# Attention with its products with v issued in one burst per chunk of queries

## The chip, the cores and the metric

The kernel runs on one core of a Trainium2 chip. The metric is the device time of one launch in microseconds (us). TensorE is called PE below, VectorE DVE, ScalarE ACT, GpSimd POOL, and SyncE, which issues the DMAs here, SP.

## What is computed

Three parts follow each other: attention with rotary embedding over 2 batches, 8 heads, 576 tokens and head size 64; a gated layer on 1152 tokens; and a layer of eight experts whose weights come from eight rounds of row and column scaling. The change is in the attention alone:

```python
scores = scale * np.matmul(q_rot, k_rot.transpose(0, 1, 3, 2))
scores = scores - np.max(scores, axis=-1, keepdims=True)
attn = np.exp(scores)
attn = attn / (np.sum(attn, axis=-1, keepdims=True) + 1e-09)
return np.matmul(attn, v).astype(np.float32)
```

## The kernel before

Attention goes through 8 pairs of heads (n = 0 to 7). A pair's 2 x 576 queries are nine units u of 128 rows: u = 0 to 3 are the two heads' first 256 queries (chunk c = 0), u = 4 holds the last 64 queries of both heads, and u = 4 to 8 make chunk c = 1.

The work of a unit u, with the short names used from here on:

- **s(u)**, L272, PE: the scores into one of two PSUM tiles of the pool ps_s (2 banks each).
- **max(u)**, L277, DVE: the negated row maximum, read from that tile.
- **exp(u)**, L293, ACT: the exponential, read from that tile, which is free afterwards.
- **t(u)**, L312, PE: four transposes of the probabilities into one of two PSUM tiles of ps_t.
- **copy(u)**, L327: that tile to SBUF, on ACT for u = 0, 2, 6 and on DVE for the others.

For each chunk there are also: **rest** (L334 to L338, PE transposes of leftover keys) with its copy **q** (L343, DVE); **spread** (L369, L371, PE) with its copy **rc** (L375, ACT), which lays out the inverse sums; the products with v, **pv** (L384, PE), five groups j = 0 to 4 of two matmuls (one per head, into the lower and the upper 64 partitions); **xf** (L393, DVE), which scales them; and, once a pair, **xh** (L399, ACT) and **xl** (L67, POOL). The operands of later pairs are made beside it: multiplications and an addition on POOL (L214, L218), the **hl cast** (L224, ACT), the **hl subtraction** (L67, DVE or POOL) and SP's DMAs that stack them (L246 to L252). The conversion of the next part's first weights (L134 to L150) also runs during pairs 2 to 4.

The order is a table: `at(step, slot, ...)`. Pair n starts at step 9n, and in each step the slots are emitted in order. On PE a step holds s(u), then t of two units earlier, then rest, then spread, then pv:

```python
SLOTS = ["load", "pe0", "dve0", "act0", "act1", "dve1", "dve2", "pe1", "pe2", "pe3", ...]
t0 = b + 5 + 5 * c
for j in range(5):
    at(t0 + VALUES[c][j], "pe3", values, n, c, j)
at(t0 + SUMMED[c], "dve3", summed, n, c)
```

So chunk 0 has its products from the step of u = 7 on, and they end in the step of the next pair's u = 0; chunk 1 has them from the next pair's u = 3 to its u = 5. PE, POOL and SP keep the written order. On DVE and ACT the scheduler moves some instructions, as the rows below show.

Of the kernel before, what the change touches and what calls it, by code (L numbers as in the profile page):

```python
# [42 lines left out]
LOAD_V = -2  # L43
REST = (1, 0)
SPREAD = (1, 2)
VALUES = ((2, 2, 4, 4, 4), (2, 2, 4, 4, 4))
SUMMED = (5, 5)
ACT_TURNS = (0, 2, 6)
CONVERSIONS = (18, 32)
# [8 lines left out]
def fused(ctx, tc, qk, v, rope, wgv, wo, wg2, w1, w2, out):  # L58
# [109 lines left out]
    def attention(xT, W):  # L168
        with ExitStack() as st:
# [236 lines left out]
            def at(step, slot, fn, *args):  # L406
                plan.setdefault((max(step, FIRST), SLOTS.index(slot)), []).append((fn, args))
# [5 lines left out]
            for n in range(pairs):  # L413
# [26 lines left out]
                for c in range(2):  # L440
# [8 lines left out]
                    for j in range(5):  # L449
                        at(t0 + VALUES[c][j], "pe3", values, n, c, j)  # L450
                    last = n == pairs - 1
# [457 lines left out]
```

## Time and profile before

| | |
|---|---|
| time, median of 3 runs | 1163.0 us (1162.06 to 1171.15) |
| profiled execution: time, span | 1172.19 us, 1170.4 us |
| PE busy | 1146.6 us, 98% of the span |
| DVE, ACT, POOL busy | 816.7, 392.3, 89.9 us |
| attention | first 174 us of the span |
| granted TensorE clock, mean of the span | 0.983 |

The page's chain of work that ended last is PE for 91% of the span. In PE's timeline each row gives start, duration, engine, line, output and inputs, shapes, and the count; a matmul of the program stands there as two records, so four transposes read x4 while four matmuls of pv read x8. A duration includes the time in which a result drains out of the array, so the distance between starts, not the duration, is what an instruction costs PE.

### The profile page before, as it was taken

How to read it: one execution, taken by the hardware profiler on the slowest of the kernel's cores; microseconds unless marked ns; L12 is line 12 of the kernel's file. 1: busy time of each engine (PE TensorE's matmuls, PEld its weight loads, DVE VectorE, ACT ScalarE, POOL GpSimd, SP SyncE). 2: the span in 40 equal slices, each digit the busy share in tenths (PEclk: the TensorE clock that was granted, in tenths of full speed). 3: DMA queues.
4: the chain of work that ended last, by engine and by line, in shares of the span. 5: the costliest groups of instructions: out<-in, count | busy, mean ns of one | idle time of the engine just before them, and what ended most of it. 6: DMA issues, size and time to landing. Idle time of an engine off the chain costs nothing.

```text
span 1170.4 us, 17008 instructions
## 1 busy us (share of the span) xinstructions
PE 1146.6 (98%) x6840; PEld 1033.4 (88%) x6840; DVE 816.7 (70%) x1420; ACT 392.3 (34%) x656; POOL 89.9 (8%) x88
## 2 busy tenths in 40 slices
PE   7999999999999998999999999999999999999998
PEld 6776768999999987998989989989899899898997
DVE  6588767997875477866857758568577585685763
ACT  4476654443432344321312213213122132131220
POOL 5467500000000000000000000000000000000000
PEclk7799999999999999999999999999999999999999
DMA  4767604332222011111111111111111111111002
GB/s 159 191 175 203 148 12 145 108 108 73 79 84 73 18 55 45 49 52 36 55 54 37 37 45 52 49 36 55 54 37 37 48 50 48 36 55 54 19 1 81
DMA packets 24991, 80.64 MB, mean 69 GB/s; under 512 B 4368, under 2 KB 4880, under 8 KB 23504
## 3 DMA queue, kind: packets, MB, share of 16 engines
q1 hardware_dynamic: 24912, 79.56, 22.7%
q8 instruction: 53, 0.87, 0.3%
q14 instruction: 26, 0.21, 0.1%
HBM read 64.80 MB, written 2.36 MB: 57 GB/s over the span
## 4 chain that ended last, share of the span: by engine, by line
PE 91%; DVE 4%; DMA 2%; issue 1%; ACT 1%; SPq 1%; POOL 0%; DVEq 0%; ACTq 0%
PE p L727 11%; PE p L725 11%; PE p L726 11%; PE s L272 4%; PE pv L384 3%; PE t L312 2%; PE po L163 2%; PE po L164 2%; PE po L165 2%; PE pg L165 2%; PE pg L163 2%; PE pv L165 2%; PE pg L164 2%; PE pv L164 2%; PE pv L163 2%
## 5 line engine op out<-in xcount | busy, mean ns | idle before, releaser
L725 PE MATMUL p<-wh,hh 128*128 128x512 f32 x576 | 224.9, 390 | 0.4 <-ACT hh L669 0.4
L727 PE MATMUL p<-wh,hl 128*128 128x512 f32 x576 | 224.5, 390 | 0.1
L726 PE MATMUL p<-wl,hh 128*128 128x512 f32 x576 | 224.4, 390 | 0.0
L100 ACT CAST wh<-raw 128x768 fp32r<-128x768 f32 (+1 forms) x96 | 94.1, 981 | 332.5 <-PE p L727 230.4
L737 DVE SCALAR_TENSOR_TENSOR acc<-p,Pm,acc 128x512 f32<-128x512 f32 x126 | 94.4, 749 | 146.6 <-PE p L727 146.6
L67 DVE TENSOR_TENSOR wl<-raw,wh 128x768 fp32r<-128x768 f32 (+1 forms) x96 | 108.4, 1130 | 36.4 <-ACT wh L100 34.9
L727 PEld LDWEIGHTS p<-wh,hl 128*128 128x128 f32 x576 | 108.1, 188 | 23.3 <-DVE hl L670 0.8
L725 PEld LDWEIGHTS p<-wh,hh 128*128 128x128 f32 x576 | 108.2, 188 | 22.6 <-ACT hh L669 0.9
L726 PEld LDWEIGHTS p<-wl,hh 128*128 128x128 f32 x576 | 108.2, 188 | 21.6
L669 ACT ACTIVATE hh<-d 128x1152 fp32r<-128x1152 f32 (+1 forms) x68 | 74.6, 1098 | 118.2 <-DVE d L674 118.2
L670 DVE SCALAR_TENSOR_TENSOR hl<-d,hh 128x1152 fp32r<-128x1152 f32 (+1 forms) x68 | 85.8, 1262 | 20.6 <-ACT hh L669 20.6
L277 DVE TENSOR_REDUCE ng<-s 128x1 f32<-128x576 f32 x72 | 54.0, 753 | 25.0 <-PE s L272 23.3
L293 ACT ACTIVATE p<-s,ng 128x576 f32<-128x576 f32 x64 | 47.6, 744 | 32.0 <-DVE ng L277 32.0
L111 DVE TENSOR_TENSOR raw<-raw 128x256 f32<-128x256 f32 x128 | 53.4, 417 | 0.6
L163 PE MATMUL pg<-xh,wh 128*128 128x384 f32 x144 | 48.9, 339 | 3.3 <-ACT wh L143 2.6
L165 PE MATMUL pg<-xh,wl 128*128 128x384 f32 x144 | 48.7, 338 | 0.0
L164 PE MATMUL pg<-xl,wh 128*128 128x384 f32 x144 | 48.6, 338 | 0.0
L164 PE MATMUL po<-ul,wh 128*128 128x384 f32 x144 | 48.4, 336 | 0.0
L165 PE MATMUL po<-uh,wl 128*128 128x384 f32 x144 | 48.4, 336 | 0.0
L163 PE MATMUL po<-uh,wh 128*128 128x384 f32 x144 | 48.4, 336 | 0.0
L164 PE MATMUL pv<-xl,wh 128*128 128x384 f32 x144 | 48.3, 335 | 0.0
L163 PE MATMUL pv<-xh,wh 128*128 128x384 f32 x144 | 48.3, 335 | 0.0
(3330 smaller groups left out, 2720.6 us busy)
## 6 DMA issues: line engine op xcount, KB each, us to landing
raw<-in_w SPq DMA_DIRECT2D x64, 512.0 KB, 3.9
raw<-in_wgv SPq DMA_DIRECT2D x11, 1024.0 KB, 4.8
x<-in_qk SPq DMA_DIRECT2D x15, 576.0 KB, 4.6
raw<-in_wo SPq DMA_DIRECT2D x12, 512.0 KB, 3.8
x<-hl SPq DMA_DIRECT2D x42, 144.0 KB, 3.4
x<-hl SPq DMA_DIRECT2D x14, 288.0 KB, 4.1
v<-in_v SPq DMA_DIRECT2D x8, 320.0 KB, 4.7
out<-acc SPq DMA_DIRECT2D x9, 256.0 KB, 2.0
```

Of the source, the lines that this page charges most:

```text
L67: (eng or nc.vector).tensor_tensor(out=out_, in0=a, in1=hi.bitcast(F32), op=ALU.subtract)
L100: nc.scalar.copy(out=hi[:, 0:n], in_=raw[:, 0:n])
L163: nc.tensor.matmul(ps, wh[wsl], xh[xsl], start=first, stop=False)
L164: nc.tensor.matmul(ps, wh[wsl], xl[xsl], start=False, stop=False)
L165: nc.tensor.matmul(ps, wl[wsl], xh[xsl], start=False, stop=last)
L277: nc.vector.tensor_reduce(out=R[n, u], in_=SC[n, u][:, :, 0:288], axis=AX.XY, op=ALU.max, negate=True)
L669: nc.scalar.activation(out=hh[:, f, ts], in_=src, func=AF.Relu)
L670: nc.vector.scalar_tensor_tensor(out=hl[:, f, ts], in0=src, scalar=0.0, in1=hh[:, f, ts].bitcast(F32), op0=ALU.max, op1=ALU.subtract)
L725: nc.tensor.matmul(po, hh[:, f, tl], wh[:, ws], start=f == 0, stop=False)
L726: nc.tensor.matmul(po, hh[:, f, tl], wl[:, ws], start=False, stop=False)
L727: nc.tensor.matmul(po, hl[:, f, tl], wh[:, ws], start=False, stop=f == 3)
L737: nc.vector.scalar_tensor_tensor(out=acc[:, t], in0=po, scalar=Pm[:, t, e:e + 1], in1=acc[:, t], op0=ALU.mult, op1=ALU.add)
```

## The change

The table VALUES gives for each of a chunk's five groups of products the step in which it is issued, counted from t0. Groups 0 and 1 go from t0 + 2 to t0 + 4, where groups 2, 3 and 4 already were.

```diff
-VALUES = ((2, 2, 4, 4, 4), (2, 2, 4, 4, 4))
+VALUES = ((4, 4, 4, 4, 4), (4, 4, 4, 4, 4))
```

On PE this is chunk 1 of pair 0, with pair 1's scores around it (p_396 and q_397 are the turned probabilities, x the stacked operands, hl and bd those of unit 4):

```order
 L371 MATMUL t<-fold,both 128x64
-L384 MATMUL pv<-p_396,v 64x320 x4
 L272 MATMUL s<-hl_273,bd_120 128x288 x6
 L312 MATMUL t<-ident,p 128x128 x4
 L272 MATMUL s<-x_288,x_296 128x288 x4
 L312 MATMUL t<-ident,p 128x128 x4
-L384 MATMUL pv<-p_396,v 64x320 x4
+L384 MATMUL pv<-p_396,v 64x320 x8
 L384 MATMUL pv<-q_397,v 64x320 x2
```

Four of the ten matmuls move behind s(4), t(2), s(5) and t(3). In chunk 0 they move in the same way behind s(8), t(6), the next s(0) and t(7). The last pair's chunk 1 already had its ten matmuls in a row, so 15 of the 16 chunks change.

On DVE the scheduler places one instruction differently. In the stretch of chunk 1 of pair 4, with pair 5's units, these rows stand before the change:

```order
L277 TENSOR_REDUCE ng<-s 128x1
L327 COPY p_1459<-t 128x4x128
L343 COPY q_1460<-rest 128x320
L277 TENSOR_REDUCE ng<-s 128x1 x2
L327 COPY p_1588<-t 128x4x128
L67 TENSOR_TENSOR hl_1522<-x,hl_1522 128x576
L352 RECIPROCAL sum<-sum 128x4
```

and these with it:

```order
L277 TENSOR_REDUCE ng<-s 128x1
L327 COPY p_1459<-t 128x4x128
L343 COPY q_1460<-rest 128x320
L67 TENSOR_TENSOR hl_1517<-x,hl_1517 128x576
L277 TENSOR_REDUCE ng<-s 128x1 x2
L327 COPY p_1588<-t 128x4x128
L277 TENSOR_REDUCE ng<-s 128x1
```

The rows are max(1), copy(8) and q, then max(2) and max(3), copy(1). The hl subtraction, which stood behind copy(1), now stands ahead of max(2). It is ahead of max(2) in the stretches of pairs 0, 1, 3, 4 and 5, behind max(2) in that of pair 2, and there is none in that of pair 6.

On ACT the same stretch read, before,

```order
L358 COPY iv<-sum 128x256
L360 ACTIVATE both<-mask,sum 128x128
L293 ACTIVATE p,sum<-s,ng 128x576
L327 COPY p_1588<-t 128x4x128
L224 CAST hl_1522<-x 128x576
L293 ACTIVATE p,sum<-s,ng 128x576
```

and now reads

```order
L358 COPY iv<-sum 128x256
L360 ACTIVATE both<-mask,sum 128x128
L224 CAST hl_1517<-x 128x576
L293 ACTIVATE p,sum<-s,ng 128x576
L327 COPY p_1588<-t 128x4x128
L293 ACTIVATE p,sum<-s,ng 128x576
```

The rows with L293 are exp(1) and exp(2). The hl cast has moved from behind copy(0) to ahead of exp(1). The rows of POOL and SP are the same in both kernels.

## Rows read from the trace of the kernel before

**Rows 1.** Windows: stretch, PE, PEld, DVE, ACT, POOL busy us, PEclk, DMA share, GB/s
```profile
20.00:45.00 25.00, 24.97 (x100) 19.01 (x98) 13.34 (x21) 11.98 (x30) 10.48 (x9) 0.50 0.61 160
...
120.00:145.00 25.00, 24.96 (x185) 18.66 (x184) 18.86 (x33) 18.52 (x47) 12.32 (x13) 1.00 0.62 154
```
**Rows 2.** Timeline of PE, s(1) of pair 5 to s(0) of pair 6
```profile
118.58 0.80 PE L272 MATMUL s<-x,x 128*128 128x288 f32 x4
...
120.01 0.78 PE L272 MATMUL s<-x,x 128*128 128x288 f32 x4
...
121.09 0.80 PE L272 MATMUL s<-x,x 128*128 128x288 f32 x4
...
122.65 1.30 PE L384 MATMUL pv<-p,v 128*64 128x320 f32 x8
123.88 1.06 PE L272 MATMUL s<-hl,bd 128*128 128x288 f32 x6
...
125.12 0.77 PE L272 MATMUL s<-x,x 128*128 128x288 f32 x4
...
128.18 0.80 PE L272 MATMUL s<-x,x 128*128 128x288 f32 x4
...
129.61 0.77 PE L272 MATMUL s<-x,x 128*128 128x288 f32 x4
130.43 0.65 PE L312 MATMUL t<-ident,p 128*128 128x128 f32 x4
131.01 1.08 PE L384 MATMUL pv<-p,v 128*64 128x256 f32 x8
132.03 0.80 PE L272 MATMUL s<-x,x 128*128 128x288 f32 x4
...
133.02 0.79 PE L272 MATMUL s<-x,x 128*128 128x288 f32 x4
```
**Rows 3.** Timeline of DVE in the same pair: max(1) to copy(4)
```profile
119.42 0.76 DVE L277 TENSOR_REDUCE ng<-s 128x1 f32<-128x576 f32 x1 [0.29 <-PE s L272]
120.09 0.68 DVE L327 COPY p<-t 128x512 f32<-128x512 f32 x1
120.69 0.48 DVE L343 COPY q<-rest 128x320 f32<-128x320 f32 x1
121.09 1.60 DVE L277 TENSOR_REDUCE ng<-s 128x1 f32<-128x576 f32 x2
...
123.20 0.75 DVE L67 TENSOR_TENSOR hl<-x,hl 128x576 fp32r<-128x576 f32 x1
...
129.69 0.68 DVE L327 COPY p<-t 128x512 f32<-128x512 f32 x1
```
**Rows 4.** Timeline of ACT in the same pair: exp(1), copy(0), exp(6) to exp(7)
```profile
120.21 0.74 ACT L293 ACTIVATE p<-s,ng 128x576 f32<-128x576 f32 x1 [1.22 <-DVE ng L277]
...
121.26 0.59 ACT L327 COPY p<-t 128x512 f32<-128x512 f32 x1 [0.22 <-PE t L312]
...
129.81 0.74 ACT L293 ACTIVATE p<-s,ng 128x576 f32<-128x576 f32 x1 [2.06 <-DVE ng L277]
...
130.79 0.68 ACT L399 CAST xh<-xf 128x576 fp32r<-128x576 f32 x1
131.37 0.68 ACT L224 CAST hl<-x 128x576 fp32r<-128x576 f32 x1
131.94 0.75 ACT L293 ACTIVATE p<-s,ng 128x576 f32<-128x576 f32 x1
```
**Rows 5.** Timeline of PE, the last pair's chunk 1, groups 0 to 3
```profile
171.05 2.39 PE L384 MATMUL pv<-p,v 128*64 128x320 f32 x16
```
**Rows 6.** Timeline of PE, chunk 0 of pair 0, groups 0 and 1, then 2 and 3
```profile
36.12 1.98 PE L384 MATMUL pv<-p,v 128*64 128x256 f32 x8
...
43.19 1.98 PE L384 MATMUL pv<-p,v 128*64 128x256 f32 x8
```
**Rows 7.** Timeline of POOL: the addition that the moved hl cast reads
```profile
118.60 1.43 POOL L218 TENSOR_TENSOR x<-x 128x576 f32<-128x576 f32 x1
```

## Prediction, made before the change was run

> **What bounds the kernel now.** I read the windows by stage first. In the steady attention (120 to 145 us) PE is busy 24.96 of 25.00 us at full clock, DVE 18.86 and ACT 18.52 [rows 1]. So PE carries the time there, but DVE and ACT are close enough that a chain through them can hold PE up for a part of a step. "Busy" doesn't show this, because short waits hide between matmuls that drain; the distances between starts do. Therefore the timelines come next, of PE [rows 2], DVE [rows 3] and ACT [rows 4], over one pair.
>
> The reader is to see one chain in them. The scores have two PSUM tiles, so s(3) can't start before exp(1) has read the tile of s(1). s(1) starts at 118.58, max(1) at 119.42, exp(1) at 120.21, s(3) at 121.09 [rows 2 to 4]: 0.84 + 0.79 + 0.88 = 2.51 us from s(u) to s(u + 2), with nothing queued in between. PE's own work in a step with no product and no rest is 0.99 us (132.03 to 133.02), so two such steps are worth 1.98 us and the chain is longer. Before the change few steps stand like that: the steps from s(3) to s(4) and from s(7) to s(8) carry the first burst, 1.23 us (122.65 to 123.88) and 1.02 us (131.01 to 132.03) [rows 2]. While PE multiplies by v, DVE and ACT catch up. The change empties just these two steps.
>
> **The bursts themselves.** It removes no matmul. Two bursts become one, and one change between scores and products less is paid per chunk. The last pair's chunk 1 already shows the merged form: 16 records take 2.39 us [rows 5], where 8 take 1.30 [rows 2]. So two bursts cost 2.60, one 2.39, and the saving is 0.21 us per chunk, 15 x 0.21 = 3.2 us if nothing else moved. Put the other way, the later burst grows by 2.39 - 1.30 = 1.09 us in chunk 1. For chunk 0 no merged form is in the trace; in proportion it grows by 1.08 x 1.09 / 1.30 = 0.91 us, with 1.02 (no saving at all) as the upper bound.
>
> **Chunk 0, walked from s(6) = 0** (128.18). exp(6) starts at 1.63, xh at 2.61, the hl cast for a later pair at 3.19, exp(7) at 3.76 [rows 4]. This queue of ACT hangs on s(6) and has the same order in the changed kernel, so exp(7) stays where it is although max(7) is done earlier. The next pair's s(0) needs its tile: 3.76 + 0.88 = 4.64. PE alone would be there sooner: s(7) at 1.43; t(5) at 2.25 as now, since it takes the PSUM tile that copy(4) empties (129.69 to 130.37 [rows 3], t(5) at 130.43 [rows 2]); then, without the burst, s(8) at 132.03 - 128.18 - 1.02 = 2.83, and s(0) 0.99 later at 3.82. So PE waits 0.82 us ahead of s(0). Before, s(0) came at 4.84. The gain is 0.20, the burst behind it grows by 0.91, net **+0.71 us**.
>
> **Chunk 1, walked from s(1) = 0** (118.58). DVE runs max(1) at 0.84, copy(8) at 1.51, q at 2.11 and is free at 2.51 [rows 3]. There max(2) stood; now the hl subtraction does, and it takes about the 0.67 us that DVE spends on max(1) (119.42 to 120.09; the row's 0.75 includes its drain) [rows 3]. max(2) starts at 3.18, exp(2) at 3.18 + 0.79 = 3.97, and s(4) at the earliest at 3.97 + 0.88 = 4.85. PE alone: s(3) at 2.51 plus 2.79 - 1.23 = 1.56, that is 4.07. So PE waits 0.78 us ahead of s(4). s(5) follows 1.24 later at 6.09; exp(3), with max(3) right behind max(2) at 3.85, needs to start by 6.09 - 0.88 = 5.21 and can. Before, s(5) came at 6.54. Gain 0.45, burst grows by 1.09, net **+0.64 us**. Where no hl subtraction is in the way, max(2) stays at 2.51, s(4) comes at 2.51 + 0.79 + 0.88 = 4.18 and s(5) at 5.42: gain 1.12, net 0.
>
> Behind max(2) on DVE stand max(3) and copy(1), and t(2) waits for copy(1)'s PSUM tile; by 4.52 + 0.60 = 5.12 it is free, while s(4)'s six matmuls, 1.06 us long [rows 2], run until 5.91, so nothing further is held. The moved hl cast on ACT goes ahead of exp(1), where ACT is idle for 1.22 us [rows 4]; I cost it at nothing as long as POOL's addition is done by then (rival C).
>
> **The sum over the chunks.** Chunk 1: pairs 0, 1, 3, 4, 5 have the subtraction ahead of max(2), 5 x 0.64 = 3.2; pair 2 has it behind, between 0 and 0.64, taken as 0.2; pair 6 has none, 0; pair 7 is unchanged. Chunk 0: pairs 1, 4, 5 at 0.71 make 2.1; in pairs 2 and 3 the weight conversion on DVE already holds PE up, so the new wait lies partly inside an old one, between 0 and 0.71, taken as 0.3 each; in pair 6 no hl cast follows xh, so exp(7) starts at 3.19, s(0) at 4.07, net 4.07 - 4.84 + 0.91 = +0.1; pair 7 has no further s(0), 0; pair 0 runs at half clock [rows 1], where PE's own steps are twice as long and the chain hides, 0. Total 3.2 + 0.2 + 2.1 + 0.6 + 0.1 = **+6.2 us**. Bounds: -3.2 (every wait hidden) and +9 (no saving per burst, and pairs 2 and 3 paying in full).
>
> What follows attention waits for the last xf, whose own chunk is unchanged, so the shift goes through to the end. The profiled execution took 1172.19 us (span 1170.4), which would become 1178.4. It is 9.2 us above the median of the runs, 1163.0; against that the forecast is 1163.0 + 6.2, or **1169 us**.
>
> **The clock in pair 0.** From 20 to 45 us PE was busy 24.97 of 25 us and the granted clock was 0.50, the lower of its levels, 1.2 GHz [rows 1]. The change gathers pair 0's chunk 0 there: the 1.98 us at 36.12 [rows 6] go behind, and the joined burst starts about 1.98 us earlier than 43.19. Beside this stands a rule: the Trainium skill, in "TensorE: Matmul & The Clock Gate", section "Why this matters for your kernels", says that keeping TensorE busy continuously brings it to full clock. By that rule a longer unbroken burst could only help; the row disagrees in so far as full busyness at 20 to 45 us did not raise the clock. The sum of +6.2 leaves the clock as it is; the other outcome is rival D.
>
> **The rivals.**
>
> A, the forecast: the emptied steps are held up by the chain through the two score tiles. 1169 us, with its own range 1164 to 1173. Chance 0.62.
>
> B: the waits don't appear, because the scheduler's new places let DVE and ACT keep up. Then only the saving is left, 1163.0 - 3.2 = 1160 us. For it: PE is the busiest engine by far. Against it: 2.51 us for two steps is read from the trace, not assumed, and ACT's queue ahead of exp(7) is unchanged. Chance 0.13.
>
> C, the slower side: the hl cast, now ahead of exp(1) on ACT, waits for POOL's addition, and the hl subtraction, now ahead of max(2) on DVE, waits for the cast; max(2) to s(4) queue behind both. Before, the addition ended 1.45 us after s(1) (118.60 + 1.43 [rows 7]) and nothing urgent stood behind it. It starts from xh, and xh comes earlier against s(1) than before by the 0.7 us of chunk 0, so it should end near 0.7; the cast (0.68) then ends at 1.4, and DVE wants it at 2.51. So it decides only once the addition ends after 2.51 - 0.68 = 1.83. If it comes at 2.8, every one of the five chunks pays 1.0 us more: +5, which gives 1174 us, and later by as much again 1179. For it: POOL carries conversion work too. Chance 0.17.
>
> D: the clock rises at the start of the joined burst in pair 0. Its 16 records take twice 1.98 us at half clock [rows 6]; at full clock half of that, 2.0 us less: 1163.0 + 6.2 - 2.0 = 1167 us. Against it: the same matmuls at 36.12 did not raise it. Chance 0.08.
>
> **How the numbers follow.** The predicted time is A's, 1169. The low end, 1161, leaves out most of B (0.10); the high end, 1177, leaves out the upper half of C (0.08). So 1161 to 1177 holds about 8 in 10. A measurement can tell about 1% of this kernel, 11.6 us, from no change: faster means below 1151.4, slower above 1174.6. No case lies below 1151; I leave 0.02 for it. Above 1174.6 lies about half of C, 0.09, and a share for the runs themselves, which differed by 9.1 us (1162.06 to 1171.15) with the same kernel, so that A's 1169 could be measured above the line: 0.10. Slower 0.19, same 0.79.
>
> **What would show it.** In the changed kernel's timeline of PE, s(6) to the next s(0) should be 4.64 us and s(1) to s(5) 6.09, s(5) to s(6) should grow from 3.06 to 4.15, and a steady pair as a whole should get 0.71 + 0.64 = 1.35 us longer. In DVE's timeline the hl subtraction should start about 2.5 us after s(1) and max(2) 3.2 after it. If s(0) comes at 3.82 and s(4) at 4.07, B holds. If max(2) starts later than 3.2 after s(1) with DVE idle ahead of the hl subtraction, C holds. If PEclk is 1.00 before 45 us, D. The forecast is wrong altogether if the scores' waits stay where they are and a steady pair gets shorter.

## The result, and the profile after

The median of 11 runs is 1171.86 us (1167.38 to 1178.65), against 1164.03 us (1162.06 to 1172.22) of 11 runs of the kernel before beside them. The ratio is 1.0058, with a 95% interval of 1.0036 to 1.0081. The change costs 7.8 us, a little over half a per cent, where +6.2 us was forecast; the median lies inside the forecast's range of 1161 to 1177.

The profiled execution took 1170.55 us, with a span of 1168.8 us and a mean granted clock of 0.991. Its page gives first the busy time of each engine, then the share of each engine in the chain of work that ended last:

```profile
PE 1138.7 (97%) x6840; PEld 1031.5 (88%) x6840; DVE 812.9 (70%) x1420; ACT 392.5 (34%) x656; POOL 89.8 (8%) x88
...
PE 87%; DVE 5%; ACT 3%; DMA 2%; issue 1%; SPq 1%; POOL 1%; DVEq 0%; POOLq 0%
```

PE carries 87% of that chain where it carried 91%: DVE has 5% (4% before) and ACT 3% (1% before). The view of waits for PE from 100 to 165 us names the place. Its columns are who waits for whom, the total in us, the times and the longest. Before, the same view is empty.

```profile
PE s L272 <- ACT p L293: 4.2, 6, 0.8
```

PE's timeline over the same pair as [rows 2], s(1) of pair 5 to s(0) of pair 6:

```profile
113.56 0.80 PE L272 MATMUL s<-x,x 128*128 128x288 f32 x4
...
116.07 0.80 PE L272 MATMUL s<-x,x 128*128 128x288 f32 x4
...
118.49 1.04 PE L272 MATMUL s<-hl,bd 128*128 128x288 f32 x6 [0.80 <-ACT p L293]
...
119.72 0.77 PE L272 MATMUL s<-x,x 128*128 128x288 f32 x4
...
120.86 2.38 PE L384 MATMUL pv<-p,v 128*64 128x320 f32 x16
...
123.85 0.80 PE L272 MATMUL s<-x,x 128*128 128x288 f32 x4
...
126.51 0.78 PE L272 MATMUL s<-x,x 128*128 128x288 f32 x4
...
128.50 0.66 PE L272 MATMUL s<-x,x 128*128 128x288 f32 x3 [0.77 <-ACT p L293]
```

The reader is to see the two emptied steps. s(4) waits 0.80 us (118.49) and the next s(0) 0.77 us (128.50), both for an exponential. The joined burst takes 2.38 us, as [rows 5] had it. s(1) to s(5) is 119.72 - 113.56 = 6.16 us, s(5) to s(6) 4.13, s(6) to s(0) 4.65.

DVE's timeline answers to [rows 3], from max(1) to max(3):

```profile
114.40 0.76 DVE L277 TENSOR_REDUCE ng<-s 128x1 f32<-128x576 f32 x1 [0.29 <-PE s L272]
...
115.67 0.48 DVE L343 COPY q<-rest 128x320 f32<-128x320 f32 x1
116.07 0.75 DVE L67 TENSOR_TENSOR hl<-x,hl 128x576 fp32r<-128x576 f32 x1
116.73 1.41 DVE L277 TENSOR_REDUCE ng<-s 128x1 f32<-128x576 f32 x2
```

The hl subtraction starts 116.07 - 113.56 = 2.51 us after s(1), with no idle time ahead of it, and max(2) 3.17 after s(1). On ACT, to set beside [rows 4], are the moved hl cast, exp(1) and exp(2), then xh, the later hl cast and exp(7):

```profile
114.34 0.67 ACT L224 CAST hl<-x 128x576 fp32r<-128x576 f32 x1 [1.28 <-POOL x L218]
115.19 0.74 ACT L293 ACTIVATE p<-s,ng 128x576 f32<-128x576 f32 x1 [0.17 <-DVE ng L277]
...
117.52 0.74 ACT L293 ACTIVATE p<-s,ng 128x576 f32<-128x576 f32 x1 [0.69 <-DVE ng L277]
...
126.46 0.68 ACT L399 CAST xh<-xf 128x576 fp32r<-128x576 f32 x1
127.04 0.68 ACT L224 CAST hl<-x 128x576 fp32r<-128x576 f32 x1
127.61 0.75 ACT L293 ACTIVATE p<-s,ng 128x576 f32<-128x576 f32 x1
```

POOL's addition, which that first cast reads [rows 7], is now this row:

```profile
112.90 1.41 POOL L218 TENSOR_TENSOR x<-x 128x576 f32<-128x576 f32 x1
```

It ends at 114.31, 0.75 us after s(1), and the cast begins at once, in time.

### The profile page after: what moved, and what is told of

It is laid out like the page before. It is cut to its first block, busy times and chain, and to the rows that moved or that the text cites. A ratio compares the mean times of both kernels' runs of the same rounds, so it can differ in the third digit from the quotient of the medians.

```text
span 1168.8 us, 17007 instructions
## 1 busy us (share of the span) xinstructions
PE 1138.7 (97%) x6840; PEld 1031.5 (88%) x6840; DVE 812.9 (70%) x1420; ACT 392.5 (34%) x656; POOL 89.8 (8%) x88
## 4 chain that ended last, share of the span: by engine, by line
PE 87%; DVE 5%; ACT 3%; DMA 2%; issue 1%; SPq 1%; POOL 1%; DVEq 0%; POOLq 0%
PE p L727 11%; PE p L725 11%; PE p L726 11%; PE pv L384 3%; PE s L272 3%; PE po L164 2%; PE po L165 2%; PE po L163 2%; PE pg L165 2%; PE pv L165 2%; PE pg L163 2%; PE pg L164 2%; PE pv L163 2%; PE pv L164 2%; ACT p L293 1%
## 5 line engine op out<-in xcount | busy, mean ns | idle before, releaser
L293 ACT ACTIVATE p<-s,ng 128x576 f32<-128x576 f32 x64 | 47.7, 745 | 37.1 <-DVE ng L277 37.1
L272 PE MATMUL s<-x,x 128*128 128x288 f32 x224 | 44.2, 319 | 6.4 <-ACT p L293 6.3
L165 PE MATMUL pv<-xh,wl 128*128 128x384 f32 x144 | 48.3, 336 | 0.0
```

The costliest lines, as they stand in the source:

```text
L165: nc.tensor.matmul(ps, wl[wsl], xh[xsl], start=False, stop=last)
L272: nc.tensor.matmul(ps[:, c, o:o + ks.stop - ks.start], q, k, start=t == 0, stop=t == len(terms) - 1)
```

## The experiments

Theory A says that the joined burst itself is cheap and that the emptied steps uncover the chain of 2.51 us through the two score tiles. Against it stand B (DVE and ACT keep up), C (a wait for POOL) and the idea that a long burst costs by itself. All durations between starts below are read in PE's timeline.

### Chunk 0 alone

```diff
-VALUES = ((4, 4, 4, 4, 4), (4, 4, 4, 4, 4))
+VALUES = ((4, 4, 4, 4, 4), (2, 2, 4, 4, 4))
```

> Only chunk 0 has its products in one burst; chunk 1 keeps its two. Theory (emptied steps are held by the chain through the two score tiles): in a steady pair s(6) to the next s(0) stays at 4.64 us and the burst behind s(0) is 0.9 us longer, so chunk 0 loses about 0.7 us a pair and the kernel about +3 us against the kernel before; chunk 1's s(1) to s(5) stays at 6.54, though the hl subtraction stands ahead of max(2) here too, since the first burst covers it. Rival (the place of the hl subtraction costs by itself): s(1) to s(5) grows, and the kernel loses about +6.

The profiled execution took 1877.68 us at a mean clock of 0.555, so its steps say nothing. The others gave 1.0062 (1.0040 to 1.0084), but from five times of 1164.27 to 1174.28 us. The same kernel in more runs:

> Chunk 0 alone in one burst, once more, since the first profile of it fell into an execution with a throttled clock. Theory: s(6) to the next s(0) is 4.64 us and the burst 0.9 us longer in pairs 1, 4 and 5; s(1) to s(5) stays at 6.54 although the hl subtraction stands ahead of max(2) in most pairs, since chunk 1's first burst covers it; in sum about +3 us in the steps. Its five undisturbed times of the first look were 1164 to 1174, more than +3: if the steps account for it, there is a wait of several us somewhere in pair 2 or 3, where the weight conversion runs; if not, the clock stood at half for longer.

Median 1166.57 us against 1164.04, ratio 1.0014 (0.9993 to 1.0036): +2.5 us, with an interval that reaches below nothing. The spread goes with the clock: the runs at a mean clock of 0.985 took 1171.4 to 1171.9 us, those at 0.993 to 0.994 took 1163.7 to 1163.9. In PE's timeline, s(6) of pair 5 and s(0) of pair 6:

```profile
120.15 0.80 PE L272 MATMUL s<-x,x 128*128 128x288 f32 x4
...
124.80 0.79 PE L272 MATMUL s<-x,x 128*128 128x288 f32 x4 [0.79 <-ACT p L293]
```

The steps are clear where the time is not: s(6) to s(0) is 4.65 us in three of the six pairs, 4.11 in pair 6, which has no hl cast behind xh, and s(0) to s(1) 3.62 where it was 2.75. In chunk 1 s(1) to s(5) stays at 6.54 to 6.83, although the hl subtraction stands ahead of max(2) here too: with a burst in the step it is covered. So the subtraction alone costs nothing in chunk 1; what the empty step costs without it, the next experiment shows. In sum the steps give less than the +3 us expected: from s(1) of pair 1 to the last product of attention it takes 129.67 us against 128.10, +1.57, mainly because chunk 0 of pair 3, beside the weight conversion, gets 0.6 us shorter.

### Chunk 1 alone

```diff
-VALUES = ((4, 4, 4, 4, 4), (4, 4, 4, 4, 4))
+VALUES = ((2, 2, 4, 4, 4), (4, 4, 4, 4, 4))
```

> Only chunk 1 has its products in one burst. Theory: s(6) to the next s(0) stays at 4.84 us as before; s(1) to s(5) shortens, and since the scheduler puts the hl subtraction behind max(2) and max(3) here, by more than in the kernel with both chunks changed: about 5.6 to 5.8 us instead of 6.16, so that chunk 1 loses only 0.1 to 0.3 us a pair, about +1 us over the kernel. Rival (a burst of ten matmuls costs by its own length, wherever the subtraction stands): s(1) to s(6) loses 0.65 us a pair as with both chunks changed, +3 to +4 us.

Median 1166.66 us against 1163.65, ratio 1.0039 (1.0021 to 1.0057), +3.0 us. DVE's timeline in chunk 1 of pair 5 shows another order, max(2), the hl subtraction, max(3):

```profile
131.41 0.74 DVE L277 TENSOR_REDUCE ng<-s 128x1 f32<-128x576 f32 x1
132.08 0.75 DVE L67 TENSOR_TENSOR hl<-x,hl 128x576 fp32r<-128x576 f32 x1
132.74 0.75 DVE L277 TENSOR_REDUCE ng<-s 128x1 f32<-128x576 f32 x1
```

There s(1) to s(5) is 5.60 us (5.61 in pair 3, 5.49 in pair 6), and the chunk costs almost nothing, so the empty step alone costs little too: s(4) waits 0.21 us, and for POOL's operand (bd, L236), not for an exponential. In pair 0 the subtraction stands ahead of max(2), and the distance is 6.16, as in the changed kernel; in pairs 1 and 2, beside the weight conversion, it is 6.19 and 6.38. The place of one instruction of 0.67 us in DVE's order is thus worth 0.56 us of PE per chunk, near the 0.64 that the prediction put between its two cases. The time rose by 3 us where about +1 was expected, and the steps account for it: from s(1) of pair 1 to the last product it takes 131.22 us against 128.10, +3.12. Some 2.0 us of that are between s(1) and s(6), mostly in pairs 0 and 2, and 0.85 behind s(6) of the last pair, where the cause wasn't separated.

### The burst one step earlier

```diff
-VALUES = ((4, 4, 4, 4, 4), (4, 4, 4, 4, 4))
+VALUES = ((3, 3, 3, 3, 3), (3, 3, 3, 3, 3))
```

> All five groups of both chunks at t0 + 3, one step earlier than in the changed kernel: again one burst per chunk, but it stands in the steps of s(8) and s(4), between the thin steps. Theory: what costs is the emptied steps side by side, not the joining, so a steady pair takes about what it took before or 0.1 to 0.3 us less (17.2 or a little under), and the kernel 0 to -2 us against the kernel before. Rival (a joined burst costs by itself, in PE or in waiting for its operands): +5 us or more, as the changed kernel.

The profiled execution took 6374.38 us and can't be read. The other five times lie in two groups, near 1167.5 us at a mean clock of 0.993 and near 1174.8 us at 0.985; ratio 1.0073 (1.0049 to 1.0096). No gain, against the expectation. The same order stands again below, with more warming.

### xh one step later

```diff
-at(ts + 1, "act1", finish, n, 0)
-at(ts + 1, "pool", finish, n, 1, slice(0, S), pool_)
+at(ts + 2, "act1", finish, n, 0)
+at(ts + 2, "pool", finish, n, 1, slice(0, S), pool_)
```

> The changed kernel with xh and xl one step later; PE's order is the same. On ACT xh now stands behind exp(7), and on DVE the scheduler puts the hl subtraction behind max(2). Theory: exp(7) starts 0.57 us earlier, at about 3.19 after s(6), so s(6) to the next s(0) falls from 4.65 to about 4.07; s(1) to s(5) falls from 6.16 to about 5.6; a steady pair gets about 1.1 us shorter than in the changed kernel, and the kernel 4 to 6 us faster than it, within 2 us of the kernel before. Rival (the wait ahead of s(0) is not ACT's queue but PE or the PSUM tiles of t): both distances stay.

Median 1169.13 us, 2.7 below the changed kernel's; against the kernel before 1.0056 (1.0043 to 1.0069). On ACT xh now stands behind exp(7):

```profile
126.64 0.74 ACT L293 ACTIVATE p<-s,ng 128x576 f32<-128x576 f32 x1
...
127.38 0.66 ACT L399 CAST xh<-xf 128x576 fp32r<-128x576 f32 x1
```

and on PE the wait ahead of s(0) shrinks from 0.77 to 0.23 us, s(6) to s(0) to 127.53 - 123.42 = 4.11:

```profile
89.11 0.80 PE L272 MATMUL s<-x,x 128*128 128x288 f32 x4 [2.77 <-ACT p L293]
...
123.42 0.80 PE L272 MATMUL s<-x,x 128*128 128x288 f32 x4
...
127.53 0.80 PE L272 MATMUL s<-x,x 128*128 128x288 f32 x4 [0.23 <-ACT p L293]
```

s(1) to s(5) also falls, to 5.53 and 5.55 in chunk 1 of pairs 4 and 5, where the hl subtraction now stands behind max(2). In pairs 0 and 3 the scheduler left it ahead of max(2), against the expectation, and the distance stays at 6.16. A pair with both distances shortened is 17.42 us where the changed kernel has 18.57 and the kernel before 17.2. That is the mechanism, twice. The total gained less than the 4 to 6 us expected, and the first row above shows a second reason: in pair 3, amid the weight conversion, s(8) waits 2.77 us, and behind it the clock falls, so that s(0) to s(1) takes 5.01 us instead of 3.62. Windows, with PE, PEld, DVE, ACT and POOL busy, then the granted clock:

```profile
90.00:94.00 4.00, 3.64 (x20) 2.60 (x20) 2.50 (x4) 3.50 (x9) 4.00 (x4) 0.57 0.45 102
```

### More warming: 40 matmuls instead of 20 ahead of the first scores

`WARM = 40` on the kernel before, on the changed kernel, and on the one with its burst a step earlier. The hope was to take the clock's scatter out.

> The kernel before with 40 instead of 20 warming matmuls ahead of the first scores, so that PE has work in most of its idle 6.33 us between 7.65 and 13.99 us. If that idle stretch is what brings the clock to half for pair 0, the granted clock stays at 1.00 through pair 0, the time falls by 2 to 8 us against the kernel before and the runs lie closer together. If not (the clock falls for another reason), the clock is 0.50 from about 12 us as before and the time is the same or up to 1 us longer.

Median 1162.68 us against 1164.25, ratio 0.9983 (0.9956 to 1.0011). The clock was not kept:

```profile
10.00:17.00 7.00, 4.92 (x43) 4.30 (x41) 6.41 (x9) 1.01 (x3) 4.17 (x4) 1.00 0.33 95
17.10:27.20 10.10, 7.93 (x32) 7.03 (x33) 5.15 (x9) 5.26 (x13) 3.18 (x2) 0.50 0.25 72
```

It is granted in full over the warming and the first scores and halves at 17 us, inside an idle stretch of PE of 3.84 us, and the median of the runs hardly moved.

> The changed kernel with 40 warming matmuls. Theory: of the 7.8 us between the two medians about 5.9 are the steps' waits and the rest is that the clock stood at half for longer in more of the changed kernel's runs. With the clock at full in both, this run is 5.5 to 7 us slower than the kernel before with 40 warming matmuls (pair 0's chunk 0 now pays its 0.7 us as well). Rival (all of the 7.8 is in the steps): 8 us or more.

Median 1169.83 us against the same 1164.25, ratio 1.0031 (1.0012 to 1.0051), and 7.15 above the kernel before with the same warming, just outside the 5.5 to 7 expected. From s(1) of pair 1 to the last product of attention it takes 135.6 us against 128.2, +7.4, of which 1.6 are again a fall of the clock behind pair 3's gap:

```profile
91.08 0.80 PE L272 MATMUL s<-x,x 128*128 128x288 f32 x4 [2.34 <-ACT p L293]
...
94.69 2.99 PE L384 MATMUL pv<-p,v 128*64 128x256 f32 x16
```

```profile
93.50:96.50 3.00, 3.00 (x16) 1.90 (x17) 1.54 (x3) 2.51 (x8) 2.92 (x3) 0.50 0.42 94
97.00:100.00 3.00, 3.00 (x27) 2.16 (x23) 1.40 (x3) 0.85 (x2) 0.30 (x1) 1.00 0.57 114
```

The burst takes 2.99 us instead of 1.95, s(0) to s(1) 5.24 instead of 3.62. The twelve times fall into two groups, 1168.28 to 1168.64 (three) and 1169.58 to 1170.29 (nine, the profiled one among them): 1.5 us apart, about what the fall costs.

> One burst per chunk at t0 + 3, with 40 warming matmuls, so that the clock does not blur it. Theory (emptied steps side by side cost, joining does not): a steady pair takes 17.0 to 17.3 us, the run is within 2 us of the kernel before with 40 warming matmuls. Rival (with the burst in the steps of s(8) and s(4) another operand or tile is late there, for example what copy or q writes, or the burst itself costs): a steady pair takes 17.7 us or more, and the run is 4 us or more slower; then the timeline shows which wait it is.

Median 1169.05 us, ratio 1.0023 (0.9996 to 1.0050), 6.4 above the kernel before with the same warming: a miss. PE from s(0) to s(4), and DVE's max(2), hl subtraction and max(3):

```profile
115.37 0.81 PE L272 MATMUL s<-x,x 128*128 128x288 f32 x4
...
116.37 0.79 PE L272 MATMUL s<-x,x 128*128 128x288 f32 x4
...
117.90 0.80 PE L272 MATMUL s<-x,x 128*128 128x288 f32 x4
...
119.21 0.80 PE L272 MATMUL s<-x,x 128*128 128x288 f32 x4
...
121.08 1.03 PE L272 MATMUL s<-hl,bd 128*128 128x288 f32 x6 [0.21 <-ACT p L293]
```

```profile
119.15 0.75 DVE L277 TENSOR_REDUCE ng<-s 128x1 f32<-128x576 f32 x1
119.81 0.75 DVE L67 TENSOR_TENSOR hl<-x,hl 128x576 fp32r<-128x576 f32 x1
120.48 0.75 DVE L277 TENSOR_REDUCE ng<-s 128x1 f32<-128x576 f32 x1
```

In chunk 0 the joined burst is free here: s(6) to s(1) is 7.58 us in both, so a burst isn't dear because it is joined. But now four steps without products, s(0) to s(3), stand in a row. DVE falls behind over them (max(2) starts 2.78 us after s(1), not 2.51) and the steps grow: s(1) to s(2) from 1.43 to 1.53 us, s(2) to s(3) from 1.08 to 1.31, and s(3) to s(4) is 1.87 where, without its burst, 2.79 - 1.23 = 1.56 would be left. A steady pair is 17.66 us, 0.47 above the kernel before. Pair 3 with the conversion costs most: 23.3 us where it was 19.6, with a gap of 3.3 us and a stretch of half clock. Moving the place of the emptied steps does not avoid the chain.

### Groups 0 and 1 left out

VALUES as before, and the loop over groups starts at 2, with group 2 now the first of the sum. The products with the first 256 of the 576 keys are left out. The line of the loop:

```diff
-for j in range(5):
+for j in range(2, 5):
```

> Groups 0 and 1 of each chunk's products with v (256 of the 576 keys) are left out, which takes PE the first bursts: 8 x 1.02 us and 7 x 1.23, about 17 us, and 1.2 in the last chunk. Theory (behind the emptied steps stands the chain through the score tiles): s(6) to the next s(0) goes only from 4.84 to 4.1 to 4.6 us and s(1) to s(5) from 6.54 to 5.4 to 6.1, so the time falls by 5 to 11 us against the kernel before. Rival (PE's own work sets the time): it falls by 16 to 19 us.

Median 1157.94 us, ratio 0.9930 (0.9905 to 0.9956): 6.3 us less. Six of the twelve runs lie at a mean clock of 0.982 to 0.985, so the steps are the better measure: from s(1) of pair 1 to the last product it takes 119.51 us against 128.10, 8.6 less, though 7 x 1.02 + 7 x 1.23 + 1.1, some 17 us of PE's work is gone there. s(6) to s(0) is 4.10 us and s(1) to s(5) 5.48 in pairs 5 and 6, as in pair 6 of the changed kernel, where neither hl cast nor subtraction is queued. With the first burst simply absent, the steps still can't be shorter than the chain; about half of the 17 us stood where PE would have waited, 0.5 of 2.25 us in such a pair and more beside the weight conversion, where pair 2 even gets 1.4 us longer, with a wait of 2.11 us and a fall of the clock behind it.

### Without the weight conversion beside attention

`CONVERSIONS = ()` on the kernel before, on the changed one, and on the changed one with xh a step later. The conversion then runs behind attention.

> The kernel before without weight conversion inside attention (it then runs at the head of the next part, which gets longer). Reference for the next two. A steady pair takes 17.2 us in all of pairs 1 to 6, with no wait ahead of the scores but 0.11 us at s(3).

> The changed kernel without weight conversion inside attention. Theory: now every pair from 1 to 5 is a steady one, with 1.3 to 1.4 us more than before, pair 6 gets 0.15 more, pair 0 0.7 to 1.4: in all 7.5 to 9 us more than the kernel before without conversion. Rival (the conversion makes a good part of the loss): 5 us or less.

> The changed kernel without weight conversion inside attention and with xh and xl one step later, so that exp(7) starts 0.57 us earlier and the hl subtraction stands behind max(2). Theory: both waits of the walk are gone or nearly, chunk 0 loses 0.1 to 0.2 us a pair and chunk 1 0 to 0.1, so the kernel is 1 to 3 us slower than the kernel before without conversion and 5 to 7 us faster than the changed one without it. Rival (in the kernel with conversion only 2.7 us of the median came back, so the two waits are not the whole cause): 2 to 3 us faster than the changed one.

Medians 1168.77, 1175.88 and 1170.79 us: the change costs +7.1 us without any conversion, and moving xh takes 5.1 of them back. At the same mean clock, 0.988, the runs of the first took 1167.7 to 1168.8 us and those of the second 1175.6 to 1176.2. A steady pair of the first takes 17.2 us in pairs 1 to 6, as expected. Windows of the three, in this order:

```profile
50.00:150.00 100.00, 99.74 (x734) 74.29 (x736) 74.10 (x129) 70.20 (x180) 56.17 (x49) 1.00 0.60 160
```

```profile
50.00:150.00 100.00, 91.60 (x684) 70.11 (x684) 67.53 (x121) 66.58 (x169) 54.45 (x47) 1.00 0.58 151
```

```profile
50.00:150.00 100.00, 98.24 (x728) 75.32 (x730) 72.96 (x128) 71.69 (x183) 54.23 (x47) 1.00 0.57 150
```

All three have the full clock in the stretch, so it plays no part there. PE is idle 0.26, 8.40 and 1.76 of 100 us. The idle time comes with the change and goes with the edit that shortens ACT's queue ahead of exp(7), while POOL is busy 54 to 56 us in all three. The same edit also puts the hl subtraction behind max(2) in all pairs but pair 0, so it shortens both queues at once; the experiment on chunk 1 alone shows DVE's by itself. From s(1) of pair 1 to the last product of attention the change takes 132.10 us against 124.44, +7.66, and with xh later 126.39, +1.95.

## Why the prediction was right, and where not

**The chain.** Right, to 0.07 us. s(6) to s(0) was to be 4.64 and is 4.65; s(1) to s(5) 6.09 and 6.16; s(5) to s(6) 4.15 and 4.13; max(2) 3.18 after s(1) and 3.17. s(0) to s(1) grows from 2.75 to 3.62, by 0.87 where 0.91 was taken. A steady pair goes from 17.20 to 18.57, +1.37 where 1.35 was forecast. The time without the conversion and the experiment on xh show the cause: it is the queue on ACT and DVE, and shortening it gives most of the time back (5.7 of 7.66 us in the steps). No run gave the scores a third PSUM tile; that the chain goes through the two tiles rests on the waits, which name exp, and on these distances.

**The sum in steps.** PE's rows for s(1) of pair 1 and the last product with v, before and then after:

```profile
46.03 0.80 PE L272 MATMUL s<-x,x 128*128 128x288 f32 x4
...
173.37 0.76 PE L384 MATMUL pv<-q,v 64*64 64x320 f32 x4
```

```profile
37.47 0.80 PE L272 MATMUL s<-x,x 128*128 128x288 f32 x4
...
170.68 0.76 PE L384 MATMUL pv<-q,v 64*64 64x320 f32 x4
```

That stretch took 128.10 us before and takes 133.97 after: +5.87, against +6.2. That the two lie so close is in part luck. Three terms were mis-sized, two down and one up, together 0.6 us less than was taken, and the other chunks, each a few hundredths dearer, make up half of that. Chunk 1 of pair 1 was taken at 0.64 and came to 0.03: before the change it already took some 0.6 us longer than in the other pairs (7.16 where they have 6.55), with PE idle for 0.39 us ahead of its spread, which the trace puts down to a copy on ACT behind an instruction of the conversion (L134), and the new wait lies inside the old one. Chunk 0 of pair 2 was taken at 0.3 and came to -0.04, that of pair 3 at 0.3 and came to 0.67. That the conversion "already holds PE up" is true of both, but in pair 3 the waits add: the longest gap was 1.05 us and is now 2.32, both ahead of s(8). DVE's timeline, with the conversion's last instruction and max(6) behind it, and PE's:

```profile
87.23 0.68 DVE L146 SCALAR_TENSOR_TENSOR raw<-raw 128x512 f32<-128x512 uint32 x1
87.83 0.75 DVE L277 TENSOR_REDUCE ng<-s 128x1 f32<-128x576 f32 x1
```

```profile
89.50 0.80 PE L272 MATMUL s<-x,x 128*128 128x288 f32 x4 [2.32 <-ACT p L293]
```

max(6) queues behind the whole conversion, and the emptied step no longer has the 1.02 us of products that covered part of that.

**The rest of the 7.8 us.** The medians differ by 7.8 us, the steps by 5.9. The remaining 2 us go with the clock, which the sum took as the same in both kernels. At equal mean clock the two kernels differ by about what the steps give: at 0.994 the runs of the changed kernel took 1167.4 and 1167.8, and runs of the kernel before, in the later experiments, 1161.2 to 1161.9; at 0.982 to 0.983 they took 1178.0 and 1178.7 against 1171.3 to 1173.0. But the changed kernel's runs are spread from 0.994 to 0.982, and most of those before lie at 0.991 to 0.994. Part of it is shown: a gap of PE that the change lengthened, with the clock's fall behind it, in the run with more warming (1.6 us). In the profiled execution of the changed kernel itself the same gap of 2.32 us passed without a fall. There the clock was at 0.50 in two stretches behind attention, 191.3 to 194.6 us and 443.9 to 447.2 us; the profiled execution of the kernel before has one (192.7 to 196.0), that of the kernel with chunk 0 alone none. So a part of the spread arises where the change touches nothing; whether the change makes such falls more frequent stays open.

**The base.** The rows of the sum come from the profiled execution of before, at 1172.19 us. It was one of the long ones: PE stood at half clock until 45.9 us, so the prediction set chunk 0 of pair 0 at nothing because of the clock. After, the clock rose at 27.4 us. The term was right, the reason not needed: with 40 warming matmuls, at full clock in both kernels, s(6) of pair 0 to s(1) of pair 1 takes 9.28 us before and 9.22 after. PE's own steps are longer in that pair, 1.67 us from s(8) to s(0) where a later pair has 0.99, so no wait shows; the expectation for the changed kernel with more warming, that the chunk would pay 0.7 us there, was wrong. Windows of before, then of after:

```profile
27.50:45.00 17.50, 17.50 (x71) 12.86 (x70) 6.99 (x11) 7.49 (x20) 7.35 (x6) 0.50 0.80 208
```

```profile
13.80:27.30 13.50, 12.13 (x50) 10.13 (x51) 11.45 (x17) 6.51 (x16) 5.75 (x7) 0.50 0.41 113
27.50:45.00 17.50, 16.70 (x127) 13.76 (x127) 12.78 (x22) 12.06 (x31) 12.24 (x12) 1.00 0.96 252
```

**The rivals.** B fell: the waits are there. C fell: the addition ended 0.75 us after s(1), near the 0.7 that was estimated and far from the deciding 1.83, and DVE was never idle ahead of the subtraction. D is not borne out. The clock did rise before 45 us, as its sign asked, but at 27.4, ahead of the change's first effect at 30.6, and it does so in the kernel before with more warming too (at 27.3). So the sign was badly chosen: the trace of one execution couldn't tell the burst's doing from the runs' own spread. The row of before just above, PE busy for 17.50 of 17.50 us at half clock, also stands against the rule of the Trainium skill ("TensorE: Matmul & The Clock Gate", section "Why this matters for your kernels") that the prediction weighed.

## What to carry to other kernels

Where two engines pass tiles back and forth, work of the busiest engine that looks fragmented may be the cover of a chain; before gathering it, walk that chain from start to start and compare it with what each step keeps. Here 0.21 us per joined burst was to be won, and with an uncovered chain of 2.51 us per two steps a loss of three times that was left. A new wait adds to an old one or hides in it, depending on which instruction is late, so price the disturbed places one by one.

## What the runs showed of the hardware

The clock was not expected to fall behind such short gaps: to 0.50 (1.2 GHz) behind 2.34 us and 2.77 us without a matmul, in the changed kernel with more warming and with xh later, and behind 2.11 us where groups 0 and 1 are left out, and back to 1.00 (2.4 GHz) by 97, 94 and 72 us. It did not fall behind 2.32 us in the changed kernel, so the length of a gap alone doesn't decide it. Nor did 40 warming matmuls keep it in the kernel before: it fell at 17 us in an idle stretch of 3.84 us, and rose near 27.3 us. And a full PE at half clock can stay there: in the kernel before it was busy 17.50 of 17.50 us without a rise, until 45.9 us.
